# Memory read and update in 32-wide TensorE tiles, with attention outputs laid out by head index and group

## Chip, cores, metric

One core of a Trainium2 chip. The metric is the time of the kernel on the device in microseconds; a kernel is run several times and the median is given.

## The reference

One transformer layer on 2048 tokens of width 1024: layer norm, attention with a memory over four segments, output projection and residual, then layer norm, a gated FFN of width 3584 and a second residual. Cut to the attention, which is what the change touches (32 heads of width 32, four segments of 512 tokens):

```python
for s in range(N):                                   # N = 4 segments
    qs, ks, vs = (q[:, :, s], k[:, :, s], v[:, :, s])
    p = softmax(qs @ ks.T * scale + mask)            # causal, within the segment
    a_dot = p @ vs
    pq = phi(qs)
    num = einsum('bhld,bhde->bhle', pq, M)           # memory read
    den = einsum('bhld,bhd->bhl', pq, z)[..., None] + 1e-06
    outs.append(g * num / den + (1.0 - g) * a_dot)
    pk = phi(ks)
    M = M + einsum('bhld,bhle->bhde', pk, vs)        # memory update
    z = z + einsum('bhld->bhd', pk)
```

Segment 0 has no memory to read, and segment 3 need not update it.

## The kernel before

Work is declared as operations with dependences and costs. A list scheduler lays out the order of every engine when the program is built; a table of shifts (444 entries, found by search) nudges its priorities. The order is then fixed. Heads lie in 8 groups of four; a half of a segment handles four groups. The eight PSUM banks are used so: 0 to 3 for the scores of the four heads of a group and later for the attention outputs, 4 for the normalisers, 5 to 7 for dense products.

The memory update made, for a group, a full 128x128 product of which only the four 32x32 blocks on the diagonal were wanted:

```python
def memory(self, s, pr):                  # pr: a pair of groups; cut
    for a in range(2):
        for kc in range(4):
            items.append((lambda gr, a=a: self.bank(gr, 0, 129, 132 * a),
                          pkn[:, a * 4 + kc, :], v[:, kc, 2 * pr + a, 0:129],
                          kc == 0, kc == 3, 129))
    ...                                   # Macc += ; Mbf = Macc * blk ; zsel = z at four columns
```

In `finish` the normalisers came first as four full products, then the attention outputs as column tiles (32 columns of the array each, four at once), with tile j for head j of one group; then each group read its memory by one full product with the block-diagonal Mbf:

```python
self.mms(gd, [(lambda gr: self.bank(gr), self.zsel[:, g0 + i, :], self.pq[:, i, :],
               i == 0, i == 3, 512) for i in range(4)], 2)
...
ins.append(e.matmul(self.ps[32 * j:32 * j + 32, b * 512 + 128 * kc:(b + 1) * 512],
                    lhsT(i, kc, j), at[i, kc][:, j, :], ..., tile_position=(0, 32 * j)))
...
m = self.mms(gm, [(lambda gr: self.bank(gr), Mb, pq, True, True, 512)], 3)   # once per group
```

The softmax here doesn't subtract the row's maximum and nothing guards it: scores larger than these inputs give would overflow.

Of the kernel before, what the change touches and what calls it, by code (L numbers as in the profile page):

```python
# [16 lines left out]

SHIFT = {
    0: (206, -1), 1: (232, 1), 2: (-346, -1), 3: (-212, 0), 4: (360, 0), 5: (-316, 0),
    6: (-273, 0), 7: (-660, 1), 8: (226, 0), 9: (-3, 1), 10: (-497, -1), 11: (-483, 0),  # L20
    12: (440, 0), 13: (-407, 0), 14: (-465, -1), 15: (-265, 0), 16: (72, 0), 17: (-1158, 1),
    18: (-419, 0), 19: (-347, 0), 20: (-798, 0), 21: (-128, 1), 22: (504, 0), 23: (-841, 0),
    24: (189, 0), 25: (242, -1), 26: (581, 0), 27: (365, 0), 28: (384, -1), 29: (-273, 0),
    30: (-144, 0), 31: (-106, 0), 32: (-294, 0), 33: (-30, 0), 34: (12, 0), 35: (-204, 0),
    36: (-459, 1), 37: (120, 0), 38: (-443, 0), 39: (-496, 0), 40: (517, 0), 41: (1079, 1),
    42: (-549, -1), 43: (120, -1), 44: (-130, -1), 45: (46, 0), 46: (-570, 0), 47: (-467, -1),
    48: (-43, 0), 49: (173, 0), 50: (-304, 0), 51: (109, 0), 52: (65, 0), 53: (-228, 0),
    54: (-49, -1), 55: (-719, 0), 56: (744, 1), 57: (-247, 0), 58: (-101, 0), 59: (495, -1),
    60: (89, 0), 61: (-171, -1), 62: (-190, 1), 63: (18, -1), 64: (229, 1), 65: (366, -1),
    66: (-309, 1), 67: (247, 0), 68: (-528, 1), 69: (545, 1), 70: (238, 1), 71: (1376, 0),  # L30
    72: (-394, 1), 73: (-22, -1), 74: (-367, 1), 75: (-88, -1), 76: (283, 1), 77: (448, 1),
    78: (186, 0), 79: (-276, -1), 80: (272, 0), 81: (-448, 0), 82: (-330, 0), 83: (-361, 0),
    84: (-167, -1), 85: (-117, 0), 86: (-126, 0), 87: (158, -1), 88: (442, 1), 89: (515, 0),
    90: (334, 0), 91: (1201, -1), 92: (309, 0), 93: (41, 0), 94: (-162, -1), 95: (-269, -1),
    96: (39, 0), 97: (934, -1), 98: (345, 1), 99: (-978, 0), 100: (663, 1), 101: (-991, 0),
    102: (-2, 0), 103: (1024, 1), 104: (-558, 0), 105: (562, -1), 106: (-1333, 1),
    107: (-926, 1), 108: (290, 0), 109: (69, 0), 110: (206, 0), 111: (29, 0), 112: (64, 0),
    113: (-681, -1), 114: (53, 0), 115: (135, -1), 116: (-261, 0), 117: (193, -1),
    118: (368, 1), 119: (-208, 1), 120: (-331, 0), 121: (620, 0), 122: (-398, 0), 123: (481, 0),
    124: (-769, -1), 125: (-1103, 1), 126: (-863, 0), 127: (323, -1), 128: (377, 0),  # L40
    129: (217, -1), 130: (682, 0), 131: (1549, 1), 132: (-866, 1), 133: (-570, 1),
    134: (-350, 1), 135: (-654, 1), 136: (188, 1), 137: (518, 1), 138: (-7, 0), 139: (-193, -1),
    140: (479, 0), 141: (-810, 1), 142: (766, -1), 143: (-627, 0), 144: (131, 0),
    145: (440, -1), 146: (-122, -1), 147: (-515, 0), 148: (174, 0), 149: (-728, -1),
    150: (-455, -1), 151: (-1008, 0), 152: (-279, 0), 153: (-1184, 0), 154: (-121, -1),
    155: (-430, 1), 156: (929, 0), 157: (310, -1), 158: (154, 0), 159: (-445, 1),
    160: (-302, 0), 161: (30, 0), 162: (305, 0), 163: (209, 0), 164: (441, -1), 165: (375, 1),
    166: (1791, 0), 167: (345, 0), 168: (397, 0), 169: (116, -1), 170: (96, 1), 171: (25, 1),
    172: (164, -1), 173: (-653, 1), 174: (-374, 1), 175: (450, -1), 176: (-866, 0),
    177: (-37, 0), 178: (-239, 0), 179: (227, 0), 180: (138, 0), 181: (167, 0), 182: (292, 0),  # L50
    183: (322, 0), 184: (196, 0), 185: (-14, -1), 186: (-338, 0), 187: (-322, 1),
    188: (-48, -1), 189: (-33, 1), 190: (225, -1), 191: (-140, -1), 192: (-847, 0),
    193: (121, 0), 194: (-409, 0), 195: (736, 1), 196: (429, 0), 197: (-1192, 0),
    198: (-478, 0), 199: (515, -1), 200: (132, 1), 201: (1124, 0), 202: (-266, -1),
    203: (522, -1), 204: (-210, 0), 205: (653, 0), 206: (450, 0), 207: (-85, 0), 208: (-878, 0),
    209: (28, 1), 210: (69, 0), 211: (-100, 0), 212: (-812, 1), 213: (338, 0), 214: (-538, -1),
    215: (-255, 0), 216: (-163, 0), 217: (299, 0), 218: (592, 1), 219: (-751, 1),
    220: (-188, 1), 221: (-284, 0), 222: (-53, 1), 223: (-89, -1), 224: (-306, -1),
    225: (283, -1), 226: (-159, 0), 227: (1549, 0), 228: (1009, 0), 229: (-347, 0),
    230: (-66, 0), 231: (-211, -1), 232: (335, 0), 233: (-131, 1), 234: (466, 0),  # L60
    235: (-945, -1), 236: (30, 0), 237: (918, 0), 238: (-402, -1), 239: (1357, 0),
    240: (-295, -1), 241: (-308, 0), 242: (-676, 0), 243: (-898, 0), 244: (276, 0),
    245: (433, 0), 246: (-313, 0), 247: (-117, 0), 248: (359, 0), 249: (-78, -1), 250: (844, 0),
    251: (1042, 1), 252: (209, -1), 253: (563, 0), 254: (-47, 1), 255: (-360, 0),
    256: (-55, -1), 257: (-614, -1), 258: (-645, 1), 259: (-26, -1), 260: (-306, 0),
    261: (-939, 0), 262: (446, -1), 263: (-644, 0), 264: (146, -1), 265: (-24, 0),
    266: (-206, -1), 267: (622, 1), 268: (-756, 0), 269: (2, 1), 270: (914, -1), 271: (524, 0),
    272: (294, 1), 273: (51, 1), 274: (-161, 0), 275: (-136, 0), 276: (220, 1), 277: (106, 1),
    278: (81, 0), 279: (196, 1), 280: (214, 0), 281: (-157, 1), 282: (95, -1), 283: (-105, 0),
    284: (180, -1), 285: (-1051, -1), 286: (-662, 0), 287: (437, 0), 288: (-25, 0),  # L70
    289: (1134, -1), 290: (944, 0), 291: (-654, 0), 292: (776, -1), 293: (10, 0),
    294: (-321, 0), 295: (-577, -1), 296: (284, 0), 297: (-196, -1), 298: (346, -1),
    299: (779, 0), 300: (629, 0), 301: (-18, -1), 302: (-645, 0), 303: (1378, 0),
    304: (344, -1), 305: (-1107, 0), 306: (484, 0), 307: (357, -1), 308: (-158, 0),
    309: (-297, 1), 310: (-66, 0), 311: (168, 1), 312: (-565, 0), 313: (-102, 0),
    314: (-93, -1), 315: (58, 0), 316: (-827, 0), 317: (-511, 0), 318: (-445, -1),
    319: (1252, 0), 320: (-382, -1), 321: (-263, -1), 322: (-41, -1), 323: (-1092, 0),
    324: (10, 0), 325: (710, 1), 326: (141, 0), 327: (-112, 0), 328: (232, -1), 329: (1039, 0),
    330: (221, 1), 331: (454, -1), 332: (208, 1), 333: (1110, 0), 334: (575, 1),
    335: (1161, -1), 336: (-685, 1), 337: (-231, 0), 338: (-232, 0), 339: (-175, 0),  # L80
    340: (877, 0), 341: (777, 0), 342: (-615, 0), 343: (430, 1), 344: (661, 0), 345: (-835, -1),
    346: (663, 0), 347: (-402, 0), 348: (354, 0), 349: (-235, 0), 350: (1064, 0),
    351: (-694, -1), 352: (1187, -1), 353: (-522, 1), 354: (572, -1), 355: (360, 1),
    356: (177, -1), 357: (289, 0), 358: (-230, 0), 359: (993, 0), 360: (-26, 1), 361: (-74, -1),
    362: (166, 0), 363: (1167, -1), 364: (-125, 0), 365: (-214, 1), 366: (339, 0),
    367: (153, -1), 368: (191, 0), 369: (-729, -1), 370: (-259, -1), 371: (-180, -1),
    372: (1204, 1), 373: (938, 0), 374: (-541, -1), 375: (342, -1), 376: (156, 0),
    377: (302, 0), 378: (121, 0), 379: (612, 0), 380: (486, 0), 381: (-112, 0), 382: (-128, 0),
    383: (305, 0), 384: (-325, 0), 385: (376, 0), 386: (644, 0), 387: (1551, 0), 388: (124, -1),
    389: (-100, -1), 390: (-565, 0), 391: (-349, 0), 392: (-54, 0), 393: (5, 0),  # L90
    394: (-1094, 1), 395: (7, 0), 396: (1, 0), 397: (3, 0), 398: (-3, 0), 399: (446, 0),
    400: (174, -1), 401: (21, 0), 402: (249, 0), 403: (31, 0), 404: (95, 1), 405: (-438, 0),
    406: (268, -1), 407: (-455, -1), 408: (-46, 0), 409: (534, 0), 410: (-47, 0), 411: (105, 0),
    412: (-1038, 1), 413: (978, -1), 414: (107, 0), 415: (18, 0), 416: (479, 0),
    417: (-267, -1), 418: (-422, -1), 419: (393, -1), 420: (230, 0), 421: (-1580, -1),
    422: (-134, 0), 423: (-688, 0), 424: (-678, 1), 425: (574, 0), 426: (-125, 0),
# [471 lines left out]
class Kernel:  # L568
# [431 lines left out]
    def attention(self, s, half):  # L1000
# [18 lines left out]
        if s < 3:  # L1019
            for pr in (2 * half, 2 * half + 1):  # L1020
                self.memory(s, pr)
# [296 lines left out]
```

## Time and profile before

| | before |
|---|---|
| median of 3 runs (range) | 903.95 us (903.93 to 904.35) |
| profiled execution, span | 901.8 us |
| TensorE busy | 896.5 us |
| VectorE, ScalarE, GpSimd busy | 423.8, 286.0, 179.9 us |
| granted TensorE clock | 1.00 |

How to read the views. The page gives each engine's busy time and the chain of work that ended last. The wait view has, for each pair of waiter and releaser, the total, the number and the longest wait. The timeline merges consecutive instructions of one kind: start, length, engine, line, operation, names, shapes, count. The recorded lengths of products in a row overlap (0.38 us each, but 0.216 from start to start; the part beyond that is called the drain here), so the cost of work on TensorE is read from one start to the next start.

### The profile page before, as it was taken

The page shows a single profiled execution, that of the slowest core. Times are in us where ns is not written, and L with a number is a line of the kernel's source. Part 1 is how long each engine was busy: PE and PEld are TensorE (multiplying, and loading weights), DVE is VectorE, ACT ScalarE, POOL GpSimd, SP SyncE. Part 2 cuts the span into 40 slices and gives each one's busy share as a digit, 9 for nine tenths or more (in the row PEclk, how much of TensorE's full clock was granted, in tenths as well). Part 3 has the DMA queues.
Part 4 walks back from the last instruction along what each step waited for, and adds up shares of the span by engine and source line. Part 5 has one row for each costly group of instructions (what it writes and reads, how often), then busy time and mean ns, then how long its engine had stood idle before and what let it go on. Part 6 is the DMA issues. An engine that isn't in the chain of part 4 may idle for free.

```text
span 901.8 us, 13023 instructions
## 1 busy us (share of the span) xinstructions
PE 896.5 (99%) x5561; PEld 408.8 (45%) x5561; DVE 423.8 (47%) x653; ACT 286.0 (32%) x306; POOL 179.9 (20%) x243
## 2 busy tenths in 40 slices
PE   8999999999999999999999999999999999999998
PEld 5444444444434444444444444444444444444445
DVE  5683868878685766564434311201343334431111
ACT  6775867686675711111211100000111111110000
POOL 2554546467473422010000000000000000000000
PEclk9999999999999999999999999999999999999999
DMA  7879672545641268554322301013123221301110
GB/s 234 215 203 276 186 151 83 153 140 118 165 117 48 71 234 222 153 155 112 94 74 67 94 30 41 24 47 94 48 76 93 71 66 52 94 24 41 37 40 30
DMA packets 146473, 96.27 MB, mean 107 GB/s; under 512 B 45424, under 2 KB 133616, under 8 KB 146416
## 3 DMA queue, kind: packets, MB, share of 16 engines
q1 hardware_dynamic: 146416, 95.45, 38.5%
q8 instruction: 44, 0.72, 0.3%
q14 instruction: 13, 0.11, 0.0%
HBM read 76.55 MB, written 8.39 MB: 94 GB/s over the span
## 4 chain that ended last, share of the span: by engine, by line
PE 99%; DMA 1%; DVE 0%; SPq 0%; issue 0%
PE ps L701 92%; PE ps L1080 4%; PE ps L1035 3%; DMA xs<-in_A_x_dram 1%; PE ps L713 0%; SPq L292 0%; DVE lnst L827 0%; DVE xnT L725 0%; DVE ob L1229 0%; DVE xs L858 0%; DVE lnve L853 0%
## 5 line engine op out<-in xcount | busy, mean ns | idle before, releaser
L701 PE MATMUL ps<-hnT,w1b 128*128 128x512 bf16 x896 | 220.0, 379 | 0.0
L701 PE MATMUL ps<-hnT,w3b 128*128 128x512 bf16 x896 | 219.1, 379 | 0.0
L1197 ACT ACTIVATE sg<-ps 128x512 bf16<-128x512 f32 x112 | 66.9, 597 | 428.8 <-PE ps L701 428.8
L701 PE MATMUL ps<-w2b,hm 128*128 128x512 bf16 (+1 forms) x924 | 196.4, 373 | 0.0
L1200 DVE SCALAR_TENSOR_TENSOR t<-sg,ps 128x512 bf16<-128x512 bf16 x112 | 76.8, 686 | 192.2 <-ACT sg L1197 192.1
L1047 ACT ACTIVATE et<-ps 128x2048 bf16<-128x2048 f32 x80 | 149.9, 1874 | 29.1 <-PE ps L1035 28.8
L701 PEld LDWEIGHTS ps<-w2b,hm 128*128 128x128 bf16 x924 | 90.4, 98 | 103.3
L701 PEld LDWEIGHTS ps<-hnT,w1b 128*128 128x128 bf16 x896 | 87.1, 98 | 105.9 <-issue 7.6
L701 PEld LDWEIGHTS ps<-hnT,w3b 128*128 128x128 bf16 x896 | 87.2, 98 | 105.6 <-issue 1.0
L1056 POOL TENSOR_SCALAR_AFFINE_SELECT et<-et 128x512 bf16<-128x512 bf16 x96 | 85.3, 895 | 86.8 <-ACT et L1047 79.7
L1205 DVE SCALAR_TENSOR_TENSOR hm<-t,ps 128x512 bf16<-128x512 bf16 x112 | 76.8, 686 | 38.2 <-PE ps L701 35.5
L1229 DVE TENSOR_TENSOR ob<-hr,ps 128x512 bf16<-128x512 bf16 (+1 forms) x33 | 22.2, 671 | 143.0 <-PE ps L701 143.0
L701 PE MATMUL ps<-xnT,wp 128*128 128x512 bf16 (+1 forms) x352 | 62.1, 321 | 0.3 <-DVE lnve L853 0.2
L701 PE MATMUL ps<-wo,oT 128*128 128x512 bf16 x256 | 61.7, 379 | 0.0
L701 PE MATMUL ps<-hnT,wp 128*128 128x512 bf16 x256 | 61.5, 380 | 0.0
L701 PEld LDWEIGHTS ps<-xnT,wp 128*128 128x128 bf16 x352 | 27.6, 98 | 25.3 <-issue 3.5
L701 PEld LDWEIGHTS ps<-wo,oT 128*128 128x128 bf16 x256 | 24.4, 98 | 29.9 <-issue 1.7
L701 PEld LDWEIGHTS ps<-hnT,wp 128*128 128x128 bf16 x256 | 23.2, 98 | 28.7 <-issue 4.1
L1134 DVE STREAM_TRANSPOSE R<-Rc 128x1024 f32<-128x1024 f32 (+1 forms) x32 | 34.5, 1094 | 0.0
L1035 PE MATMUL ps<-qT,kT 32*128 32x128 bf16 (+3 forms) x512 | 31.7, 301 | 0.0
L701 PE MATMUL ps<-wp,hnT 128*128 128x512 bf16 x128 | 31.3, 380 | 0.0
L701 PE MATMUL ps<-wp,xnT 128*128 128x512 bf16 x128 | 31.0, 380 | 0.0
(85 smaller groups left out, 547.3 us busy)
## 6 DMA issues: line engine op xcount, KB each, us to landing
w3b<-in_B_w_dram SPq DMA_DIRECT2D x28, 512.0 KB, 3.9
w1b<-in_B_w_dram SPq DMA_DIRECT2D x28, 512.0 KB, 4.0
wp<-in_A_wv_dram SPq DMA_DIRECT2D x8, 1024.0 KB, 5.5
wp<-in_A_wq_dram SPq DMA_DIRECT2D x7, 1024.0 KB, 5.9
wp<-in_A_wk_dram SPq DMA_DIRECT2D x7, 1024.0 KB, 6.0
w2b<-in_B_w_dram SPq DMA_DIRECT2D x7, 1024.0 KB, 5.6
xs<-in_A_x_dram SPq DMA_DIRECT2D x16, 256.0 KB, 5.3
h<-in_A_x_dram SPq DMA_DIRECT2D x16, 256.0 KB, 3.3
```

The source lines that it names most:

```text
L701: return [e.matmul(p[0](gr), p[1], p[2], start=p[3], stop=p[4]) for p in part]
L1035: ins.append(e.matmul(self.bank(gr, j, 512 - 128 * kc, off), k[r, g0 + g, 128 * kc:128 * kc + 128], q[r, g0 + g, 128 * kc:512], start=True ...
L1047: return [e.activation(et[:, :, :], src, AF.Exp, scale=self.scale)]
L1056: self.pool_op(lambda e, v=v, pat=pat: e.affine_select(v, v, pattern=pat, compare_op=ALU.is_ge, fill=0.0, base=0, channel_multiplier=-1), ...
L1080: ins.append(e.matmul(self.ps[32 * j:32 * j + 32, b * 512 + 128 * kc:(b + 1) * 512], lhsT(i, kc, j), at[i, kc][:, j, :], start=kc == 0 and ...
L1134: sp = self.dve_op(lambda e, dst=dst, src=src: e.transpose(dst, src), dve_ns(512 * nr), [Rc[:, i, 0:nr, :]], [rs], 2)
L1197: self.g.op("act", act_ns(512), lambda e, gr, sg=sg: [e.activation(sg, self.bank(gr), AF.Tanh, scale=0.5)], writes=[sg], cls=0, group=gg)
L1200: e.scalar_tensor_tensor(t1, sg, 1.0, self.bank(gr), op0=ALU.add, op1=ALU.mult)], reads=[sg], writes=[t1], cls=0,
L1205: e.scalar_tensor_tensor(dst, t1, 0.5, self.bank(gr), op0=ALU.mult, op1=ALU.mult)], reads=[t1], writes=[dst], cls=0,
L1229: self.g.op("dve", dve_ns(n), lambda e, gr, hs=hs, ob=ob, n=n: [e.tensor_tensor(ob, hs, self.bank(gr, 0, n), op=ALU.add)], reads=[hs], wri ...
```

## The change

The intent is to take out TensorE work whose result was thrown away or that used a quarter of the array. A PSUM bank now belongs to a head index j, and its four blocks of 32 partitions to the four groups. That allows three things. The normaliser product of group i writes only its own block, so four groups run at once as column tiles. The memory read of 4 heads in 4 groups is sixteen independent 32x32 tiles (rows by head, columns by group) that run at once. The memory update computes only the wanted blocks, as column tiles of 33 columns (32 of v and one of ones). The rows of wo are loaded in an order that matches. The read moves to behind the fourth score unit of the next half, into the score banks, and the table of shifts was searched anew.

```diff
-                              pkn[:, a * 4 + kc, :], v[:, kc, 2 * pr + a, 0:129],
-                              kc == 0, kc == 3, 129))
+                        ins.append(e.matmul(
+                            self.ps[32 * j:32 * j + 32, b + 33 * i:b + 33 * i + 33],
+                            pkn[:, 4 * i + kc, 32 * j:32 * j + 32], v[:, kc, g0 + i, j, 0:33],
+                            start=kc == 0, stop=kc == 3, tile_position=(0, 32 * j),
+                            skip_group_check=True))
 ...
-            self.mms(gd, [(lambda gr: self.bank(gr), self.zsel[:, g0 + i, :], self.pq[:, i, :],
-                           i == 0, i == 3, 512) for i in range(4)], 2)
+                for i in range(4) if zsel else ():
+                    ins.append(e.matmul(
+                        self.ps[32 * i:32 * i + 32, b * 512:(b + 1) * 512],
+                        self.zsel[:, g0 + i, :], self.pq[:, i, :], start=True, stop=True,
+                        tile_position=(0, 32 * i), skip_group_check=True))
 ...
-            m = self.mms(gm, [(lambda gr: self.bank(gr), Mb, pq, True, True, 512)], 3)
+                return [e.matmul(self.ps[32 * i:32 * i + 32, gr.banks[j] * 512:gr.banks[j] * 512 + 512],
+                                 self.Mbf[32 * j:32 * j + 32, g0 + i, :],
+                                 self.pq[32 * j:32 * j + 32, i, :], start=True, stop=True,
+                                 tile_position=(32 * j, 32 * i), skip_group_check=True)
+                        for i in range(4) for j in range(4)]
```

(Cut: buffers, masks, layout of v and wo, evacuations, the new table of shifts.)

## The prediction

> **What bounds the kernel now.** I read the page's busy shares, then the chain of work that ended last, then the waits of TensorE, and then the TensorE timeline inside the attention stage, because that is where the change lies.
>
> ```profile
> PE 896.5 (99%) x5561; PEld 408.8 (45%) x5561; DVE 423.8 (47%) x653; ACT 286.0 (32%) x306; POOL 179.9 (20%) x243
> ...
> PE 99%; DMA 1%; DVE 0%; SPq 0%; issue 0%
> ```
>
> TensorE is busy for 896.5 of 901.8 us, and 99% of the chain that ended last is TensorE itself. A busy TensorE is not yet a full one, so the next view asks what it waited for.
>
> ```profile
> PE ps L701 <- DVE oT L766: 1.2, 1, 1.2
> PE ps L713 <- DVE xs L858: 1.1, 2, 0.7
> PE ps L701 <- DVE lnve L853: 0.2, 1, 0.2
> ```
>
> Those are all of its waits: 2.5 us, all in the start-up. (Columns: total us, times, longest us.) The timeline shows whether the stream between is dense. Columns: start, length, engine, line, operation, count.
>
> ```profile
> 105.19 1.03 PE L701 MATMUL ps<-hnT,wp 128*128 128x512 bf16 x4
> 106.15 0.40 PE L1035 MATMUL ps<-qT,kT 32*128 32x128 bf16 x8
> 106.48 1.04 PE L701 MATMUL ps<-hnT,wp 128*128 128x512 bf16 x4
> 107.35 1.03 PE L701 MATMUL ps<-pq,zsel 128*128 128x512 bf16 x4
> 108.22 1.03 PE L701 MATMUL ps<-hnT,wp 128*128 128x512 bf16 x4
> ...
> 119.45 0.62 PE L701 MATMUL ps<-v,pkn 128*128 128x129 bf16 x8
> 119.90 1.89 PE L701 MATMUL ps<-wp,hnT 128*128 128x512 bf16 x8
> ...
> 125.85 2.35 PE L1080 MATMUL ps<-et,ones 128*32 128x512 bf16 x64
> 128.02 1.26 PE L1080 MATMUL ps<-et,v 128*32 128x512 bf16 x32
> ...
> 133.56 0.38 PE L701 MATMUL ps<-pq,Mbf 128*128 128x512 bf16 x1
> 133.78 1.03 PE L701 MATMUL ps<-wo,oT 128*128 128x512 bf16 x4
> ```
>
> The lengths contain the drain, which the next work overlaps; what an operation takes from TensorE is start to next start. Four normaliser products (zsel) take 108.22 - 107.35 = 0.87 us, 0.217 each. One memory read (Mbf) takes 133.78 - 133.56 = 0.22. Eight memory-update products (pkn) take 119.90 - 119.45 = 0.45. A mode change costs about 0.1 us: four dense products ahead of scores take 106.15 - 105.19 = 0.96 instead of 0.87. There are no holes: dense work of the next segment's projections and the output projection fills each gap. So this is a sum of TensorE time. A microsecond of TensorE work taken out is a microsecond off the end, as long as the filler does not run out, and nothing done on another engine counts by itself.
>
> **What the Trainium skill says.** "TensorEngine Tiling (Array Packing)", Tiling Modes, Key Properties: tiles work independently, and changing the tiling mode drains TensorE. The trace agrees: column products run four at once (64 in 128.02 - 125.85 = 2.17 us, where their lengths 512, 384, 256 and 128 run singly would be four times that), and the change of mode costs the 0.1 us found above. "TensorE: Matmul & The Clock Gate", Part 3, Measured speedup vs the span model: a pack lasts one matmul plus about 4 ns per further tile, and 16 tiles of 512 columns took 660 ns as one pack by itself. No 32x32 tile runs in the kernel before, so the trace is silent. The same page, "Wait — 56ns, not 53.3ns?": start to start never falls below some 25 ns however small the matmul; and, LDWEIGHTS: a load takes its columns divided by 1.2 GHz, 27 ns for 32. The trace has no matmul narrower than 128 columns to confirm or refute either.
>
> **The change part by part.**
>
> (1) Normaliser read. Removed: segments 1 to 3, two halves, so 6 groups of four full 512-column products, 6 x 0.87 = 5.2 us. Added: the same four as column tiles, which run at once, 6 x 0.22 = 1.3 us, put at the head of the existing column run, so no new mode change. Gain 3.9.
>
> (2) Memory read. Removed: 24 full products, which lay in the dense stream without a mode change, 24 x 0.22 = 5.3 us. Added: 6 packs of sixteen 32x32 tiles. One pack streams 512 columns, 0.22, plus 15 x 4 ns from the skill = 0.28 us as an estimate; and it stands alone between other modes, so I add a change in and a change out, 0.2. 6 x 0.48 = 2.9 us. Gain 2.4.
>
> (3) Memory update. Removed: 12 groups of eight 129-column products (three segments, four pairs of groups), 12 x 0.45 = 5.4 us; three quarters of their output was thrown away by the block mask. Added: 6 groups of 16 rounds of four column tiles, 33 columns wide, directly behind the column run, so no new mode change. What a round costs is the one figure I cannot read. Array time is 33/2.4 = 14 ns, and the skill's load of 32 columns is 27 ns. From above: in the 2.17 us of 64 column products are 4 sets whose streaming is 1280 columns, 533 ns at the 2.4 GHz that 512 columns in 0.216 us imply. A set took 542 ns, so at most 9 ns is overhead, and the 128-wide round with its four weight loads fits in 53 + 9 = 62 ns. I choose 41 ns, the middle between 27 and 55. 6 x 16 x 41 = 3.9 us. Gain 1.5.
>
> (4) The other engines. The two evacuations of the update become one (402 ns each for 258 elements before), the block-mask product becomes a copy on GpSimd, the three or four small zsel writes become one. The broadcast transposes (1228 ns), the products with gcol (745 ns) and the final additions keep their number and width. VectorE was 79% busy between 140 and 180 us (31.61 of 40), and this lightens it a little. TensorE hid all of that, so it is worth 0.
>
> (5) Order. The read moves to behind the fourth score unit of the next half, in the four score banks; the output projection of segment 1 moves behind it; the table of shifts is retuned. The filler is the same. Outside the attention stage, which is over by 345 us, the FFN and its weight traffic are not touched, so two thirds of the span stays as it is.
>
> Sum: removed 5.2 + 5.3 + 5.4 = 15.9; added 1.3 + 2.9 + 3.9 = 8.1; net 7.8 us. 903.95 - 7.8 = 896.2. The old order leaves practically no wait to win, a new one can only equal that or lose a little; I add 0.4 us for it: **896.6 us**.
>
> **The rivals.**
>
> *The small matmuls are bound by issue.* If 25 ns is a floor for every instruction and not for every tile, the 64 update products take 1.6 us a half instead of 0.66, that is 5.6 us more in all, and the sixteen reads take 0.40 instead of 0.28. The gain falls to about 1.5 us: some 902.5. For it: column products now average 34 ns each, so no long run in the trace goes below 25. Against it: four products of 128 columns got through in at most 62 ns, though the queue ahead of them may have been filled during the longer ones. I give it one in eight, with smaller shares of it more likely.
>
> *The score banks become the bound.* The read now holds the four banks of the scores while VectorE evicts four times, 4 x 0.745 = 3.0 us, and no score can start meanwhile. Ten score units a half come about every 3.0 us (a unit's exponential is 1.87 us, TensorE's part 0.33), so some 0.6 us of slack per unit or 6 us a half exists. One lost slot of 3 us fits in it. If it did not, attention would stretch by up to 3 us in each of six halves; this costs time only if TensorE then has no dense filler, and FFN products already fill in from 265 us on in the kernel before. At worst I expect 3 us: 899.5.
>
> *The packs do not overlap with their neighbours.* With the skill's 660 ns for a lone pack instead of 0.28 plus changes of 0.2, 6 x 0.18 = 1.1 us more: 897.7.
>
> *A gain of over 2%.* This needs 18.1 us. All removed products together are 15.9 us, so even with free replacements it is not reached. Only fewer mode changes could add: there are 80 score units and 8 column runs, two changes each, 176 x 0.1 = 17.6 us; but each unit needs all four banks, which the exponential must empty first, so two cannot stand side by side.
>
> **Range and chances.** The terms for the update (41 ns, between 27 and 60) move the result by -1.3 to +1.8 us, the packs by about 1, the order by -0.5 to +2. The low end is 894.0 and the high end 900.0. Faster by over 2%: 0.01. Slower by over 2% would take 18 us of new waits on TensorE: 0.02. Within 2%: 0.97.
>
> **What would show it.** TensorE should still be 99% of the chain and its busy time should fall by about 8 us; the span of FFN work after 380 us should be as long as before. Start to next start in the timeline: about 0.22 us for the four new zsel tiles, 0.3 for the sixteen tiles plus two changes of 0.1, 0.6 to 0.7 for the 64 update products. If the update run lasts 1.0 us or more, step 3 is wrong and the issue rival is right. Waits of TensorE on VectorE or ScalarE that add to more than 2 us after 20 us would make the bank rival right. A gain of over 10 us would mean that retuning took out something that I hold to be fixed.

## The result

| | before | changed |
|---|---|---|
| median (range), 6 runs each | 904.38 us (903.93 to 904.92) | 896.70 us (895.84 to 897.58) |
| ratio of the fast runs, 95% interval | | 0.9915 (0.9902 to 0.9927) |
| profiled span | 901.8 us | 895.0 us; run again 895.5 us |

A ratio is the mean time of one kernel's fast runs over the mean of the other's of the same rounds, so it is not quite the ratio of the medians. The prediction was 896.6 us.

The page of the changed kernel, busy times:

```profile
PE 880.6 (98%) x5833; PEld 403.4 (45%) x5921; DVE 417.6 (47%) x631; ACT 287.9 (32%) x306; POOL 173.8 (19%) x226
```

The busy time seems to fall by 15.9 us, but that is a trap: 5833 products stand against 5921 weight loads. 88 records are missing, and where they are, TensorE looks idle (its wait view has 19 waits for "issue" of at most 0.2 us, 3.0 us in all). So I ran the same kernel again for a second profile (first experiment below); its records are complete. Its page, busy times and chain:

```profile
PE 887.9 (99%) x5921; PEld 403.5 (45%) x5921; DVE 417.5 (47%) x631; ACT 287.8 (32%) x306; POOL 173.8 (19%) x226
...
PE 98%; DMA 1%; issue 0%; DVE 0%; SPq 0%
```

The true fall is 896.5 - 887.9 = 8.6 us. Its waits of TensorE, against the three of before:

```profile
PE ps L720 <- DVE xs L862: 2.1, 2, 1.2
PE ps L985 <- issue: 1.3, 1, 1.3
PE ps L708 <- DVE oT L773: 1.2, 1, 1.2
PE ps L708 <- DVE lnve L857: 0.2, 1, 0.2
```

The start-up wait of the first transposes is 2.1 instead of 1.1 us, and there is one new wait of 1.3 us for "issue", that is, for nothing that the profile shows, inside a memory update (L985). (The profiles of the kernels below with missing records show some 3 us of such short waits too; they are not counted as stops.) The timeline of the same run, one column run and one memory read:

```profile
130.55 1.81 PE L1107 MATMUL ps<-et,v 128*32 128x512 bf16 x48
132.19 0.39 PE L1100 MATMUL ps<-pq,zsel 128*32 128x512 bf16 x4
132.41 2.35 PE L1107 MATMUL ps<-et,ones 128*32 128x512 bf16 x64
134.58 0.72 PE L1107 MATMUL ps<-et,v 128*32 128x512 bf16 x16
135.12 0.70 PE L985 MATMUL ps<-v,pkn 128*32 128x33 bf16 x64
135.75 1.04 PE L708 MATMUL ps<-wo,oT 128*128 128x512 bf16 x4
...
146.78 2.10 PE L708 MATMUL ps<-wo,oT 128*128 128x512 bf16 x9
148.82 0.43 PE L1184 MATMUL ps<-pq,Mbf 32*32 32x512 bf16 x16
149.19 1.68 PE L708 MATMUL ps<-hnT,wp 128*128 128x512 bf16 x7
```

Four normaliser tiles take 132.41 - 132.19 = 0.22 us. A read of sixteen tiles takes 149.19 - 148.82 = 0.37 with the mode change out, and the change in is 148.82 - 146.78 less nine products of 0.216, 0.09: together 0.46. 64 update products take 135.75 - 135.12 = 0.63 with the mode change out, 0.53 without, so 33 ns a round of four.

The balance of this run, in us: removed 15.9; added normalisers 6 x 0.22 = 1.3, reads 6 x 0.46 = 2.8, updates 6 x 0.53 = 3.2, the stop in an update 1.3, the start-up 1.0. Net 15.9 - 9.6 = 6.3, and the spans differ by 901.8 - 895.5 = 6.3. The busy time agrees: 15.9 less the 7.3 of added work is 8.6. The medians differ by more (7.2 to 7.7), because the two profiled executions lie on opposite sides: that of before took 903.54 us, 0.4 under its median, and that of the changed kernel 897.25 us, the slowest of its five.

### The profile page after: what moved, and what is told of

Its sections match the earlier page's. It is cut to its first block, busy times and chain, and to the rows that moved or that the text cites. A ratio compares the mean times of both kernels' runs of the same rounds, so it can differ in the third digit from the quotient of the medians.

```text
span 895.0 us, 13604 instructions
## 1 busy us (share of the span) xinstructions
PE 880.6 (98%) x5833; PEld 403.4 (45%) x5921; DVE 417.6 (47%) x631; ACT 287.9 (32%) x306; POOL 173.8 (19%) x226
## 4 chain that ended last, share of the span: by engine, by line
PE 97%; issue 1%; DVE 1%; DMA 1%; ACT 0%; SPq 0%; ACTq 0%; DVEq 0%
PE ps L708 89%; PE ps L1107 4%; PE ps L1057 3%; DMA xs<-in_A_x_dram 1%; PE ps L985 0%; PE ps L1184 0%; ACT et L1069 0%; PE ps L1100 0%; DVE t L1260 0%; DVE hm L1265 0%; PE ps L720 0%; SPq L299 0%; DVE R L1163 0%; ACT sg L1257 0%; DVE Nsb L1171 0%
## 5 line engine op out<-in xcount | busy, mean ns | idle before, releaser
L708 PE MATMUL ps<-xnT,wp 128*128 128x512 bf16 (+1 forms) x345 | 59.7, 320 | 1.4 <-issue 0.6
L708 PE MATMUL ps<-hnT,wp 128*128 128x512 bf16 x250 | 59.0, 380 | 0.7 <-issue 0.6
L1200 POOL TENSOR_TENSOR oT<-Nsb,R 128x512 bf16<-128x512 f32 x23 | 35.8, 1569 | 4.1 <-DVE R L1197 4.1
L1163 DVE STREAM_TRANSPOSE R<-Rc 128x1024 f32<-128x1024 f32 x28 | 33.6, 1222 | 0.1
L1229 DVE TENSOR_TENSOR h<-h,ps 128x512 bf16<-128x512 bf16 x32 | 21.7, 680 | 25.1 <-PE ps L708 24.9
```

Source lines behind the costliest of these rows:

```text
L708: return [e.matmul(p[0](gr), p[1], p[2], start=p[3], stop=p[4]) for p in part]
L1163: return self.dve_op(lambda e: e.transpose(out, src), dve_ns(1024), [Rc[:, t, 2 * n:2 * n + 2, :]], [dst], 2)
L1200: self.either(lambda e, out=out, Ns=Ns, R1=R1: e.tensor_tensor(out, Ns, R1, op=ALU.add), 512, 2, [Ns, R1], [out], 2)
L1229: self.g.op("dve", dve_ns(512), lambda e, gr, hs=hs: [e.tensor_tensor(hs, hs, self.bank(gr), op=ALU.add)], reads=[hs], writes=[hs], cls=1, ...
```

## The experiments

The theory: the time is a sum of TensorE work, and the change takes some out. Rivals: the small products are bound by issue; the score banks become the bound; the gain belongs to the new order. Unless the text says otherwise, the order of the instructions on every engine was compared with that of the changed kernel and is the same. "The changed kernel" means 896.7 us, its median in both calls in which it ran (896.70, 896.68); before had 903.93 to 904.38 in all calls. (In the other calls the changed kernel itself did not run; there a difference below about 0.5 us means nothing.)

### The changed kernel once more

No edit.

> The changed kernel once more, unedited, for a second profile. In its first profile two waits of TensorE stand that the kernel before did not have: 0.8 us more in the start-up (a load of the input landed later) and one stop of 1.2 us inside a memory-update run. If both are chance, neither is in this profile at its place, and the span is 1 to 2 us below 895.0. If they belong to the order of the instructions, both are there again. The time against the kernel before should be 7 to 8.5 us less either way.

Measured: 896.68 us (895.9 to 897.25), ratio 0.9916. The stop in the update run is there again at the same place, now 1.3 us (1.1 in the first profile); so it belongs to the program. The start-up delay was also there again. With the same order the kernels below had 0.6 to 2.4 us in its place, so how much of it is chance stays open. The span did not fall.

### The update three times over

```diff
-            for i in range(4):
+            for i in [0, 1, 2, 3] * 3:
```

> The 64 narrow products of each memory update are issued three times over (the repeats overwrite with the same values, the result stays right); six updates, so twelve more runs of 64. Theory of the prediction, mended by the first profile: such a run takes 16 rounds of 33 ns, 0.53 us, so 12 x 0.53 = 6.4 us more than the changed kernel. With the prediction's own 41 ns a round: 7.9 us more. Rival (25 ns for every product): 1.6 us a run, 19 us more. Second rival (the stop of 1.2 us is instruction supply): more stops of that kind appear, as three times as many instructions pass in a row.

Measured: 923.71 us, 27.0 more than the changed kernel. All three numbers miss. Two views say where it went: the waits, and one window of the busy-time table (columns: window and length, busy us and count of PE, PEld, DVE, ACT and POOL, then granted clock, DMA share, GB/s).

```profile
PE ps L985 <- issue: 15.3, 7, 4.8
...
97.00:110.00 13.00, 8.20 (x326) 5.31 (x325) 6.14 (x11) 2.48 (x4) 0.47 (x2) 0.87 0.67 165
```

The products themselves are not slower: the 192 of the third update run take 2.03 us to the next dense start, of which 0.4 is a stop and 0.1 the mode change, so 0.51 us for 64, and 12 more runs of 64 are some 6 us. 15.3 us are stops for "issue", seven of them, up to 4.8 us; the changed kernel has 1.3. And a long stop can cost twice: the granted clock, 1.00 everywhere in the changed kernel, reads 0.50 from 58.5 to 65.3 us, from 106.3 to 109.7 and from 297.4 to 300.8, each time from the last part of a stop or just behind it (the stops of 4.1, 4.8 and 2.5 us) and back at 1.00 afterwards. TensorE worked in some 11.6 of these 13.7 us, which makes about 5.8 us lost, an estimate. Length alone does not decide it: in the 36-pair kernel below the clock fell behind a stop of 2.2 us and stayed at 1.00 through one of 3.05. With another stop of 1.4 us behind an update run (in the scores), the stops are 15.4 us more than in the changed kernel, and the start-up wait is 1.5 less: 6.1 + 15.4 + 5.8 - 1.5 = 25.8 of the 27.0 us. The second rival, instruction supply, is what grew.

### Blocks of instructions shifted

If TensorE's instructions come in blocks and one comes late, the stop must sit at a fixed count of instructions from the start. So I put pairs of load and product ahead of everything, in the warm-up products that run while the input loads.

```diff
-        o = self.mms(gr, [(..., w, True, True, 512)] * n, 0, split=n)
+        k = 4 if n > 1 else 1        # 36 more pairs; with 2 for 4, 12 more
+        o = self.mms(gr, [(..., w[:, 0:512 // k], True, True, 512 // k)] * (k * n), 0, split=k * n)
```

(Cut: a line that keeps the cost told to the scheduler the same.)

> As before with 24 warm-up products of 256 columns, 12 more pairs ahead instead of 36. Theory (late block): the stop moves by at least the 12 pairs, or goes, within its run; the time lies between the changed kernel and 1.5 us below it. Rival: nothing changes.

> The twelve warm-up products of 512 columns at the start become 48 of 128 columns: 36 more pairs of load and product ahead of everything else, in time that TensorE spends waiting for the input anyway; all else is the same instruction for instruction. Theory (the stop of 1.3 to 1.5 us in the fifth update run is a block of instructions that arrives late, and hits where a block begins inside a run of narrow products): the stop moves or goes, and without it the kernel is 1 to 1.5 us faster than the changed kernel. Rival (the stop comes from the data or the semaphores of that update): it stays in the fifth update run.

(The stop is in the sixth update run, not in the fifth; the texts miscounted.) First the changed kernel in its second profile, then the kernel with 12 more pairs, then that with 36 more:

```profile
269.43 0.51 PE L985 MATMUL ps<-v,pkn 128*32 128x33 bf16 x42
271.29 0.32 PE L985 MATMUL ps<-v,pkn 128*32 128x33 bf16 x22 [1.35 <-issue]
```

```profile
269.55 0.39 PE L986 MATMUL ps<-v,pkn 128*32 128x33 bf16 x30
271.64 0.41 PE L986 MATMUL ps<-v,pkn 128*32 128x33 bf16 x34 [1.70 <-issue]
```

```profile
98.04 1.11 PE L1108 MATMUL ps<-et,v 128*32 128x512 bf16 x23
102.20 0.50 PE L1108 MATMUL ps<-et,v 128*32 128x384 bf16 x9 [3.05 <-issue]
```

With 12 more pairs ahead, the stop comes after 30 products of the run and not after 42: exactly 12 earlier. (The first profile of the changed kernel also has 42.) With 36 more it is gone from that run, and a longer stop stands behind the second update run instead. So the stop is tied to the count of instructions. The busy-time table from the start to within the stop says the same (columns as above): the changed kernel, and the kernel with the read three times over (below), which has 96 more pairs ahead of that place:

```profile
0.00:270.50 270.50, 266.28 (x2631) 121.23 (x2631) 178.61 (x282) 178.89 (x166) 122.95 (x166) 1.00 0.67 174
0.00:272.50 272.50, 267.96 (x2759) 122.65 (x2759) 179.14 (x284) 178.85 (x166) 123.04 (x167) 1.00 0.68 173
```

2631 weight loads have been issued at the stop, and 2631 also with 12 more pairs ahead, with full normalisers and in both kernels "with the order unchanged" below; with the read three times over the stop has left the update run and stands in the column run behind it, at 2759, which is 128 pairs or 256 instructions later. The Trainium skill, "Runtime: NRT & Kernel Launch", Instruction fetch mechanics, says that instructions come in blocks of 16 KiB, 256 instructions, by a DMA queue of the engine's own. The traces agree: in each of these windows the DMA view has a packet of an "instruction" queue of that size. For the window of the stop in the changed kernel (268 to 272 us; columns: packets, MB, share):

```profile
q8 instruction: 1, 0.02, 1.8%
```

The number of its packets fits too: 44 in the kernel before, 47 in the changed one and 53 with the update three times over, where loads and products together are 43.4, 46.3 and 52.3 times 256. And the packed traces show what each stop waited for: in the changed kernel the packet landed at 269.93 us and TensorE went on at 271.29. All 21 stops for "issue" of 0.2 us or more, in eleven profiles, end so, 1.3 to 1.5 us (once 1.7) behind the landing of a packet of this queue.

A dense product uses two instructions in 0.216 us, so a block lasts 27.6 us. An update run uses 128 in 0.53 us, half a block. That page also holds that the fetch is hidden by the pace of issue; in such a run it is not. Why a packet comes late in one run and not in another stays open. In the two longest stops, of 4.8 and 4.1 us, its transfer began only 2.3 and 1.7 us after TensorE had stopped, and in both the data queue had been busy until shortly before (over 90% from 97 to 103.3 us, and from 51.3 to 57.1); that fits an instruction packet that waits behind data, but I did not test it.

The times: 12 more pairs 898.37 us (ratio 0.9938), 36 more 902.12 us (0.9972). Both are slower than the changed kernel, the first by little: each has a second stop (0.7 us at 98 us, and 2.2 us at 59), and with 36 more pairs the clock is at 0.50 from 59.3 to 62.7 us. Two of the five runs of that kernel, at 900.06 and 900.92 us, show a clock of 1.00 throughout, the other three 0.998. The stop can be moved but I did not find a place where it costs nothing. My hope of a faster kernel fell; that the stop is a block of instructions that comes late is shown.

### The read three times over

```diff
-                        for i in range(4) for j in range(4)]
+                        for _ in range(3) for i in range(4) for j in range(4)]
```

> Each memory read issues its sixteen 32x32 tiles three times over (result stays right); six reads, so twelve more packs. Theory: a pack streams like one product of 512 columns, 0.22 to 0.28 us, so 2.6 to 3.3 us more than the changed kernel, and the two mode changes around it do not grow. Rival (a pack does not overlap with the next and takes 0.66 us): 7.9 us more. If the tiles ran four at once only: 0.87 us a pack, 10 us more.

Measured: 899.61 us (898.8 to 900.46), 2.9 more. Twelve packs, so 0.24 us each. Its timeline:

```profile
148.90 0.92 PE L1184 MATMUL ps<-pq,Mbf 32*32 32x512 bf16 x48
149.75 2.55 PE L708 MATMUL ps<-hnT,wp 128*128 128x512 bf16 x11
```

0.85 us for three packs against 0.37 for one: 0.24 for each further one, about one product's worth. Sixteen tiles do run at once and packs follow each other without a drain. The lone-pack rival (7.9 us) and four-at-once (10 us) are out.

### The normaliser as full products again

```diff
-                        self.ps[32 * i:32 * i + 32, b * 512:(b + 1) * 512],
-                        self.zsel[:, g0 + i, :], self.pq[:, i, :], start=True, stop=True,
-                        tile_position=(0, 32 * i), skip_group_check=True))
+                        self.ps[:, b * 512:(b + 1) * 512],
+                        self.zsel[:, half, 128 * i:128 * i + 128], self.pq[:, i, :],
+                        start=i == 0, stop=True, skip_group_check=True))
```

(Cut: zsel made wide with zeros between, and the norm statistics' buffer halved to make room.)

> Part one undone: the normaliser product is four full-width products of 512 columns that add into the bank, as in the kernel before, instead of four column tiles at once; the rest stays. Theory (a sum of TensorE time): 6 x (0.87 - 0.22) = 3.9 us more than the changed kernel. Rival (the gain comes from the new order of the work, the parts are hidden): within 1 us of the changed kernel.

Measured: 900.95 us (900.28 to 901.5), 4.3 more. The theory said 3.9, the rival under 1. In the timeline of this kernel:

```profile
132.87 1.04 PE L1100 MATMUL ps<-pq,zsel 128*128 128x512 bf16 x4
133.84 2.36 PE L1107 MATMUL ps<-et,ones 128*32 128x512 bf16 x64
```

0.97 us instead of 0.22, a mode change back into column tiles included, as the full products here stand in the middle of the column run; the change into them, 0.11 more, lies ahead of this line. So it is in four of the six halves, 0.86 each; in the other two the normaliser is the head of the column run, with no mode change added, and costs 0.64 more. Together 4.7 us, against 4.3 by the clock. So the cost on TensorE accounts for this part's gain.

### The read four at once

The read with weights of full height, zero outside the head's block, so it needs column tiles only.

```diff
-                                 self.Mbf[32 * j:32 * j + 32, g0 + i, :],
-                                 self.pq[32 * j:32 * j + 32, i, :], start=True, stop=True,
-                                 tile_position=(32 * j, 32 * i), skip_group_check=True)
-                        for i in range(4) for j in range(4)]
+                                 self.Mbf[:, g0 + i, j, :],
+                                 self.pq[:, i, :], start=True, stop=True,
+                                 tile_position=(0, 32 * i), skip_group_check=True)
+                        for j in range(4) for i in range(4)]
```

The first version made the weights with four small GpSimd instructions that the scheduler was told of:

> Part two cut back: the sixteen products of a memory read have the full height of 128 rows, with weights that are zero outside the head's block, so that they run as column tiles, four at once in four rounds, and not sixteen at once. Place, banks and evictions stay. Theory (TensorE time): 4 x 0.22 = 0.87 us instead of 0.22 to 0.28 for each of six reads, 3.6 to 3.9 us more than the changed kernel. Rival (a lone pack costs its mode changes and its drain whatever is in it): under 2 us more.

Measured: 928.71 us, 32 more. The extra operations had changed the whole order, and one wait shows what that did:

```profile
PE ps L708 <- DMA h<-in_A_x_dram: 14.3, 2, 9.9
```

TensorE stood for 14.3 us at the output projection, which had nothing to do with the read. So this run says nothing about the question, and I built it again with one GpSimd instruction in the old one's place, and with the order unchanged:

> The four-at-once read again, now with the weights made by one GpSimd instruction whose cost the layout of the order is not told, so every engine runs the same instructions in the same order as in the changed kernel. Theory (TensorE time): 6 x (0.87 - 0.22) = 3.9 us more than the changed kernel, so about 900.6. Rival (the 32 us of the first try belonged to the read itself): above 920.

Measured: 902.71 us (902.36 to 903.58), 6.0 more. In its timeline a read is

```profile
149.11 1.05 PE L1187 MATMUL ps<-pq,Mbf 128*32 128x512 bf16 x16
150.09 0.60 PE L708 MATMUL ps<-hnT,wp 128*128 128x512 bf16 x2
```

150.09 - 149.11 = 0.98 against 0.37, so 6 x 0.61 = 3.7, the theory's 3.9. Another 1.8 us are waits of scores for VectorE (1.1 and 0.7 us) and 0.3 a wait of a dense product for it. But the 1.1 us stand at 59 us, long before the first read at 149: they come from how the weights are made. In the timeline of this kernel:

```profile
55.66 2.46 POOL L1012 TENSOR_TENSOR Mbf<-Macc,hmask 128x512 bf16<-128x512 f32 x1 [1.74 <-DVE Macc L1000]
55.96 2.44 DVE L958 TENSOR_SCALAR phe<-phe 128x1024 bf16<-128x1024 bf16 x1
```

The GpSimd instruction takes 2.46 us where the old one took 0.29, and the VectorE instruction beside it 2.44 where it took 0.36 in the changed kernel; the scores behind wait. The other 1.0 us stand 5 to 9 us behind three of the reads; whether the reads or the GpSimd instructions cause them is not shown. So TensorE work explains 3.7 of the 6.0 us, the making of the weights 1.1, and 0.2 I can't assign; what the rival asked for, over 920 us, belonged to the order.

### Score banks held longer

```diff
+                    e.tensor_scalar(self.junk[:, :], self.bank(gr, j), 1.0, None, op0=ALU.mult),
                     e.scalar_tensor_tensor(R1, self.bank(gr, j), gcol, R1, ...
```

First with the doubled cost told to the scheduler:

> Each of the four evictions of a memory read is preceded by a second VectorE pass over the same bank into a spare buffer, so the four score banks stay taken for about 4 x 0.7 = 2.8 us longer, six times, and VectorE works 17 us more. The order is laid out anew with that cost. Theory (TensorE is the bound and always finds dense work): within 1 us of the changed kernel. Rival (the score banks are the bound since the reads sit in them): up to 6 x 2.8 = 17 us more.

Measured: 931.20 us, 34.5 more, beyond either. As with the four-at-once read the order was laid out anew under a table that was searched for another program, so it can't be read as the cost of the banks. With the cost not told, and the order unchanged:

> The four doubled evictions again, with the cost not told, so the order of every engine is that of the changed kernel and only 2.8 us of VectorE work is put into each of six reads. Theory (the slot after a read has slack, the order was what hurt): 0 to 4 us more than the changed kernel, as a fixed order can't refill a wait. Rival (score banks are the bound): 10 to 17 us more, in waits of TensorE at the scores behind each read.

Measured: 903.59 us (902.84 to 903.99), 6.9 more, between the two. The waits view of this run has

```profile
PE ps L1058 <- DVE R L1199: 3.3, 5, 1.0
```

that is, scores behind five of the reads wait for VectorE, up to 1.0 us each (behind the sixth, at 444 us, there are no scores left). Another 1.8 us are waits of dense products for VectorE and GpSimd; the rest I can't assign. Of 6 x 2.8 = 17 us put in, 6.9 came through. So the order has about 10/6 = 1.7 us of slack behind a read on average, an estimate. In the changed kernel itself no such wait stands (its four waits are shown above), so the banks are not its bound, but they are near.

### Both kernels in plain order

```diff
-SHIFT = { ... }
+SHIFT = {}
```

> The kernel before with an empty table of shifts, so in the order that the plain priorities give. The other half of the pair with the changed kernel in its plain order. If the table is worth nothing this equals the kernel before; I expect 1 to 15 us more, as waits of TensorE on VectorE or ScalarE come back.

> The changed kernel with an empty table of shifts. Theory (the gain is less TensorE work): it stays 6 to 10 us below the kernel before in its plain order, or the waits of either pair differ visibly in the profile. Rival (the gain is the retuned table): the two plain orders differ by less than 3 us.

Measured: before 905.93 us (905.73 to 906.66), changed 900.37 us (899.53 to 900.54). So the pair differs by 5.6 us, just under the theory's 6 to 10 and well above the rival's 3. The table is worth 2.0 us to the kernel before and 3.7 us to the changed one. What the changed kernel lacks without its table is seen in its waits:

```profile
PE ps L622 <- DVE t L1174: 3.2, 5, 1.6
```

Most of the gain is there without any table, so it is the work; the rest of it could be kept only because the order was fitted again.

## Why the prediction was right

- *The time is a sum of TensorE work.* Right. Work put back on TensorE came back in the time nearly one to one, with its order unchanged: the normaliser 4.7 us by the timeline and 4.3 by the clock, two more reads 2.9 and 2.9.
- *(1) Normaliser.* Right: 0.22 us a half. In four of six halves it stands inside the column run and not at its head, which makes no difference.
- *(2) Read.* Right: 0.46 us against 0.48, with the two mode changes as taken from the scores.
- *(3) Update.* Near in the sum for the wrong reason. A round takes 33 ns and not 41, which saves 6 x 16 x 8 ns = 0.8 us, and a stop of 1.3 us in one of the six runs, which I did not think of, takes it back: 4.5 us in all against 3.9. The issue rival in its form (25 ns for each product) is out, as a product takes 8 ns; but instruction supply does cost time, in blocks and not by the product. What holds a round at 33 ns, with an array time of 14, no run here tells apart.
- *(4) Other engines.* Right: no wait of TensorE on them is new outside the start-up.
- *(5) Order.* Half right. No wait on another engine came back, as with the new table that I had counted on; without tables the gain is 5.6 us. The 0.4 us that I allowed for the order stand against 1.0 us of start-up. And attention is not over by 345 us: the last read moved to 438 us, where before it stood at 343. The tail is as long as I said: the last 2107 products take 449.1 us before and 449.0 after.
- *The rivals.* The packs overlap fully, so that rival is out. For the score banks I had argued 6 us of slack a half from the distance of the scores (my own figures, 3.0 - 1.87 - 0.33, give 0.8 us a unit and so 8, not 6); loading them showed about 1.7 us behind each read. The outcome held since the read itself needs none of it.
- *What would show it.* I asked for a fall of TensorE's busy time of about 8 us. The first page shows 15.9, from missing records; the complete one 8.6. The run of 64 update products (0.63 us with the change out) and the lone read with its changes (0.46) came near the forecast 0.6 to 0.7 and 0.5.
- *The range.* Its terms add up to 893.8 and 901.4 us, not to 894.0 and 900.0; the measured time lies in both.

That the predicted and the measured time agree within 0.1 us is luck: the terms were off by up to 1.3 us in both directions, and the kernel before had 903.95 us when I predicted and 904.38 in the result.

## What to carry to other kernels

When TensorE is the whole chain and its timeline has no holes, cost a change by start-to-start times and ignore the other engines until something shows them; check first that the records are complete, by comparing the counts of products and weight loads. Cutting work into very narrow products saves array time but spends instructions, and a run of 64 or 192 of them can outpace their supply, as here: look for waits on "issue" inside such runs, and for the landing of an instruction packet just before each ends. A table tuned for one program can lay out a slightly edited one badly (928.7 us against 902.7 for the same read with the order kept), so an experiment on such a kernel must keep the order fixed or drop the tuning on both sides. And a helper instruction on another engine can cost more than the thing tested: look where in time a wait stands before giving it a cause.

## What the Trainium skill lacked or had wrong

- "Runtime: NRT & Kernel Launch", Instruction fetch mechanics: it says that the fetch is hidden as dispatch is slower than the refill. Here it is not: with 128 instructions in 0.53 us TensorE stopped for 1.3 us in one run of six, and for 15.3 us in all where the runs were three times as long. Its block of 256 instructions itself fits (packets of 16 KB; the stop moved by exactly the 12 pairs put ahead). No page that I found says how long after its landing a block can be used: here TensorE went on 1.3 to 1.5 us later (once 1.7).
- "TensorE: Matmul & The Clock Gate", Wait — 56ns, not 53.3ns?: it gives a floor of 25 ns from start to start and makes no exception for tiles (Part 3 of the page does have them start closer). Here it does not hold across column tiles: 64 products of 33 columns, each with its own weight load, took 0.53 us, 8 ns each; four at once in 33 ns.
- The same page, Part 3, Measured speedup vs the span model: 660 ns for sixteen tiles (the row names no columns; I take the 512 of the rows above it). Here the recorded span of a pack of 512 columns, drain included, was 0.43 us, and a pack in a row of packs cost 0.24 us. Its formula fits: one such product is recorded with 0.385 us, so 0.385 + 15 x 0.004 = 0.445, an estimate. Only the figure of 660 does not.
- "TensorEngine Tiling (Array Packing)", Tiling Modes: it names the drain at a mode change but gives no figure. Here a change took about 0.1 us (0.09 to 0.13) each way, between full, row, column and 32x32 mode.
- Pages on the notification block say that records can be lost, but none that I found says that a profile's missing product records make TensorE look idle: 88 of 5921 records missing took 7.3 us from its busy time (880.6 against 887.9 us).
